# Forming the low parts of w2 and of later q/k weights on GpSimd, with w2 spread over the steps and the first MLP product four units sooner

## The chip, the cores and the metric

One core of a Trainium2 chip runs the kernel. Its engines are TensorE (PE in the profile; PEld is its weight load), VectorE (DVE), ScalarE (ACT), GpSimd (POOL) and SyncE (SP), which here issues every DMA. Each engine works through its own instruction stream in order; semaphores tie the streams together. The metric is the device time of one execution in microseconds (us), lower is better. The kernel before takes 837.43 us, the median of three runs (837.27 to 838.78).

## The reference, cut to what matters

Sequence 2048, width 640, 32 heads of 20, a causal window of 256, an MLP of width 1536 with squared relu. Attention and MLP both read the normalized input, and the MLP's output gates the attention's:

```python
xn = _layernorm(x, axis=-1)
s = _A_ref(xn, A_wqkv, A_wo)       # windowed softmax attention, then @ wo
g = _silu(_B_ref(xn, B_w1, B_b1, B_w2, B_b2))   # relu(xn @ w1 + b1)**2 @ w2 + b2
return x + s * g
```

Everything is float32. The kernel reaches that accuracy with half-precision products: each operand is scaled by a power of two and kept as a high part `hi` (rounded to f16) and a low part `lo` (what rounding left out), and a product is three matmuls, hi*hi, hi*lo and lo*hi.

## The kernel before, in words

**Three stages.** The first (to about 119 us) normalizes x, transposes it, makes the values, the first group of q and k, and the parts of w1. The second is one loop of 269 steps (line 1023, `for s in range(steps)`), which is written out by hand: on PE, ACT, DVE, GpSimd and SP the instructions run in the order in which the Python code issues them. The third, after the loop, is the output projection with the gate.

**A step.** Sixteen pairs of heads times sixteen blocks of 128 queries give 256 steps, plus 13 in which the pipeline runs out. Step s does, for different blocks: `scores` (PE, L558) and `maxima` (DVE, L569) of block s; `scores_t` (PE, L605), `exps` (ACT exponential, L610, then the two GpSimd selects L611 and L613 that zero what lies outside the window) of block s-10; `high` (ACT, L618) of block s-11; `low` (DVE, L624, the low part of the probabilities) of block s-12; `values` (PE, L638) of block s-13. So a select is read by the `high` of the next step, and that by the `low` of the step after.

**The filler.** Between these pieces `fill` (L1007) draws matmuls from one long generator, `filler` (L888), until a quota of cost is used up: 1.58 cost units a step (423.4 units over 268 steps). The generator is a list of units: 32 `group_unit`s (q and k of groups 1 to 4, four column blocks, 15 matmuls of 0.218 each, 3.27 units), 96 `hidden_unit`s (the first MLP product, 15 of 0.111, 1.665 units) and 96 `out_unit`s (the second product with w2, 12 of 0.138). Before, the first 16 group units stand alone and the other 16 are merged evenly with the 12 hidden units of the first token block (L892); then hidden units of the next block are merged with out units of this one. What a unit leaves in PSUM is moved out by an `evac`, run by `flush` in the step: for a group L80 on ACT and L81 on DVE, for a hidden unit L848 and L849 on ACT, L851 on DVE, L852 on GpSimd.

**Pieces of weights.** Weights that are needed later come in pieces of 128 x 640 f32. `piece` (L753) puts one in `queue`; `start_pieces`, called from `issue` twice a step, takes it out, starts its DMA into one of three `raw` buffers (RAW, L39) and puts it in `started`; `tick`, called once a step after `flush`, releases at most one piece, in order, two steps or more after its DMA was issued (AGE, L718), and runs its work. Tags name the pieces: "g2" to "g4" the q and k weights of a group (two pieces each, `split_s`), "s" the 17 that are only squared and summed for a scale (12 of w2, 5 of wo, L776), "20", "21", "22" the 12 of w2 (`split_s`), "o" those of wo. A tag in `shut` isn't released. `ensure` (L745) runs what is left of a tag at once.

**split_s** (L124) is the work of a weight piece: ACT writes `hi` with a scale (L125), and DVE computes src*scale - hi into `lo` in one instruction (L126).

**When.** Group g+1 is queued when `group_unit` enters (g, block 0, q), shut until (g, block 1, q). The squares are queued at (1, 1, q); `ensure("s")` and a small product of scales come at (3, 0, q); `second_scales` (L784: two small matmuls, a chain of small DVE and GpSimd instructions) and the queueing of w2 at (3, 1, q). The first `out_unit` calls `ensure` for w2's three tags.

Of the kernel before, what the change touches and what calls it, by code (L numbers as in the profile page):

```python
# [11 lines left out]
AF = mybir.ActivationFunctionType  # L12
ALU = mybir.AluOpType

P = 128
# [8 lines left out]
NB = 4  # L24
# [33 lines left out]
def attn_mlp_kernel(ctx: ExitStack, tc, x, wqkv, wo, w1, b1, w2, b2, out):  # L58
# [91 lines left out]
    def totals(name, r, acc, k=1):  # L150
        nc.tensor.matmul(r, onesf, acc, start=True, stop=True)
        t = col(name, k)
        nc.vector.tensor_reduce(out=t, in_=r.rearrange("p (k n) -> p k n", k=k), op=ALU.add, axis=mybir.AxisListType.X)  # L153
        nc.vector.tensor_scalar(t, t, TINY, None, ALU.max)
        return t

    sc_g, qkw, w1t, mlp, esc = {}, [], [], {}, []

# [559 lines left out]
    AGE = 2  # L718
    held = [0]
    shut = set()  # L720

    def start_pieces(n=3):
        k = 0
# [7 lines left out]
    def release(n, force=False):  # L731
        done = []
        while started and len(done) < n:
            tag, at_, go = started[0]
            if not force and (tag in shut or state[2] < at_ + AGE):
                break
            done.append(started.pop(0)[2])
        return done

# [10 lines left out]
                f()  # L750
                held[0] -= 1

    def piece(tag, src, go):  # L753
        def start():
            raw = wgt.tile([P, D], F32, tag="wraw", bufs=RAW, name="raw")
            if len(src.shape) == 3:
                raw = raw.rearrange("p (c n) -> p c n", n=src.shape[-1])
            nc.sync.dma_start(raw, src)
            return lambda: go(raw)
        queue.append((tag, start))  # L760

    def queue_group(g):
        r = {}
        for i, w in enumerate("qk"):
            hi, lo = (qkw[0][:, g % 2, i, j] for j in range(2))
            off = (0 if w == "q" else D) + g * P
            piece(f"g{g}", wqkv.rearrange("(c p) n -> p c n", p=P)[:, :, off:off + P], lambda raw, hi=hi, lo=lo, w=w: split_s(hi, lo, raw, sc_g[w]))
            r[w] = (hi, lo)
        return r

# [25 lines left out]
    def queue_w2(j):  # L796
        def go(raw, f):
            if len(w2t) == j:
                w2t.append(w2p.tile([P, SLOT], F16, name=f"w2_{j}") if j == 2 else bigp.tile([P, SLOT], F16, tag="big", name=f"w2_{j}"))
            hi, lo = (lin1(w2t, (2 * f + q) * D, D) for q in range(2))  # L800
            split_s(hi, lo, raw, mlp["s2"][:, f:f + 1])
        for f in range(4 * j, 4 * j + 4):
            piece(f"2{j}", w2[f * P:(f + 1) * P, :], lambda raw, f=f: go(raw, f))

# [4 lines left out]
    def group_unit(g, b, w):  # L809
        if w == "q":  # L810
            if b == 0:
                ensure(f"g{g}")
                if g + 1 < KC:
                    ws[g + 1] = queue_group(g + 1)
                    shut.add(f"g{g + 1}")
            if b == 1:
                shut.discard(f"g{g + 1}")
                if g == 1:
                    queue_squares()
            if g == KC - 2 and b == 0:  # L820
                ensure("s")
                weighted_squares()
            if g == KC - 2 and b == 1:
                second_scales()
                for j in range(3):
                    queue_w2(j)
# [61 lines left out]
    def filler():  # L888
        groups = [(group_unit, g, b, w) for g in range(1, KC) for b in range(NB) for w in "qk"]
        hid = [[(hidden_unit, n, fc) for fc in range(NF)] for n in range(nblk)]  # L890
        mlp2 = [[(out_unit, n, tt, nh, third) for tt in range(2) for nh in range(2) for third in range(3)] for n in range(nblk)]
        half = len(groups) // 2  # L892
        units = groups[:half] + merge(groups[half:], hid[0])
        for n in range(nblk - 1):
            units += merge(hid[n + 1], mlp2[n])
        units += mlp2[-1]
# [215 lines left out]
```

## Time and profile before

| what | value |
|---|---|
| runs of the kernel | 837.27, 837.43, 838.78 us |
| the profiled execution | 837.25 us, of which 835.5 us is the span from the first to the last instruction |
| granted TensorE clock | 0.998 of full speed |
| first and last score matmul (L558) | 119.2 and 727.3 us from the span's start |
| squares of pieces (L776) | 17, from 134.8 to 173.7 us |
| splits of w2 (L125 on ACT) | 12, from 223.6 to 255.3 us |

The page's first part gives the busy time of each engine over the span; a stage view (busy time between two moments, with instruction counts) is needed to see where an engine is short, since the stages differ. DVE's line L569 runs twice a step, and each of the two is followed by a readout that the profile counts under the same line, so four instructions of L569 are one step: that makes it a clock for the steps. Durations of neighbours on ACT and DVE overlap by about 0.1 us when they follow without a gap, so busy time is a little more than what an engine needs.

### The profile page before, as it was taken

What the parts mean: (1) busy time and instruction counts of PE and PEld (TensorE: products, weight loads), DVE (VectorE), ACT (ScalarE), POOL (GpSimd) and SP (SyncE); (2) the same over time, 40 slices, a digit from 0 to 9 for tenths busy, and PEclk for the clock granted to TensorE, in tenths of its full rate; (3) what the DMA queues carried; (4) which work ended last, traced back from release to release, by engine and by line L of the source; (5) the groups of instructions that cost most, each with busy time, mean ns of one, the idle gap of its engine ahead of it and who ended that gap; (6) DMA issues with size and microseconds to landing.
All of it is one profiled execution on the core that took longest, in us unless ns stands there. A gap on an engine that the chain in (4) does not pass through costs nothing.

```text
span 835.5 us, 24908 instructions
## 1 busy us (share of the span) xinstructions
PE 815.3 (98%) x9426; PEld 548.1 (66%) x9426; DVE 686.0 (82%) x1897; ACT 648.5 (78%) x1028; POOL 476.9 (57%) x874
## 2 busy tenths in 40 slices
PE   8999999999989999999999999999999999999998
PEld 6765563445545557777777777777777777767775
DVE  6777576788999889888988889888988889875665
ACT  5456455998898989898898989898898989893321
POOL 2000001446777768797878878797887878770000
PEclk9999999999999999999999999999999999999999
DMA  6894447765463332212121212211121131055873
GB/s 240 253 342 123 146 147 255 232 183 158 145 197 119 100 102 79 52 49 66 50 68 58 67 49 54 56 60 50 54 89 45 55 97 46 10 199 181 309 288 129
DMA packets 100497, 104.51 MB, mean 125 GB/s; under 512 B 42520, under 2 KB 72856, under 8 KB 100376
## 3 DMA queue, kind: packets, MB, share of 16 engines
q1 hardware_dynamic: 100376, 102.91, 39.5%
q8 instruction: 74, 1.21, 0.6%
q14 instruction: 47, 0.39, 0.2%
HBM read 65.67 MB, written 36.83 MB: 123 GB/s over the span
## 4 chain that ended last, share of the span: by engine, by line
PE 82%; ACT 7%; DVE 5%; issue 3%; DMA 2%; SPq 0%; DVEq 0%; ACTq 0%
PE hps L689 19%; PE yps L874 19%; PE wops L689 8%; PE ops L638 7%; PE vps L292 7%; PE sps L558 7%; PE qkps L689 7%; PE stps L605 3%; PE qkps L503 3%; ACT p L610 2%; DVE junk L569 2%; ACT ph L618 1%; PE otp L956 1%; PE tps L256 1%; DVE pl L624 1%
## 5 line engine op out<-in xcount | busy, mean ns | idle before, releaser
L610 ACT ACTIVATE p<-stps,ebias,esc 128x768 f32<-128x768 f32 (+2 forms) x256 | 242.3, 947 | 50.2 <-PE stps L605 42.4
L569 DVE CUSTOM_DVE_ANT_0 junk<-sps,mask 128x320 bf16<-128x320 f32 (+2 forms) x512 | 221.3, 469 | 54.8 <-PE sps L558 44.6
L624 DVE TENSOR_TENSOR pl<-p,ph 128x768 f16<-128x768 f32 (+2 forms) x256 | 243.6, 952 | 4.7 <-ACT ph L618 4.0
L611 POOL TENSOR_SCALAR_AFFINE_SELECT p<-p 128x256 f32<-128x256 f32 x256 | 171.4, 670 | 90.4 <-ACT p L610 87.8
L618 ACT ACTIVATE ph<-p 128x768 f16<-128x768 f32 (+2 forms) x256 | 203.2, 794 | 1.9 <-POOL p L613 0.9
L689 PE MATMUL hps<-xT,w 128*128 128x256 f16 x1440 | 188.8, 273 | 0.0
L874 PE MATMUL yps<-w,hh 128*128 128x320 f16 x1152 | 186.6, 300 | 0.0
L689 PEld LDWEIGHTS <-w 128*128 128x128 f16 x1440 | 133.3, 98 | 43.7 <-issue 23.7
L874 PEld LDWEIGHTS <-hh 128*128 128x128 f16 x1152 | 105.1, 98 | 55.6 <-issue 21.8
L689 PE MATMUL qkps<-xT,qkw 128*128 128x512 f16 x480 | 117.0, 381 | 0.8 <-DVE w_t L153 0.8
L613 POOL TENSOR_SCALAR_AFFINE_SELECT p<-p 128x256 f32<-128x256 f32 x224 | 110.5, 493 | 0.0
L558 PE MATMUL sps<-ks,qs 60*64 60x320 f16 (+2 forms) x1024 | 86.1, 313 | 6.5 <-DVE mt L569 5.9
L638 PE MATMUL ops<-vp,ph 128*128 128x41 f16 x1440 | 89.8, 181 | 0.0
L638 PE MATMUL ops<-vp,pl 128*128 128x41 f16 x1440 | 89.5, 181 | 0.0
L638 PEld LDWEIGHTS <-ph 128*128 128x128 f16 x1440 | 84.6, 96 | 6.2 <-issue 0.6
L638 PEld LDWEIGHTS <-pl 128*128 128x128 f16 x1440 | 78.9, 96 | 5.8
L605 PE MATMUL stps<-qs,ks 62*64 62x320 f16 (+4 forms) x1024 | 79.6, 291 | 2.3 <-ACT p L610 2.0
L574 POOL CAST mp<-mt 128x8 f16<-128x8 f32 x64 | 44.1, 689 | 62.2 <-DVE mt L569 61.6
L689 PEld LDWEIGHTS <-qkw 128*128 128x128 f16 x480 | 41.6, 98 | 53.4 <-issue 11.7
L852 POOL TENSOR_TENSOR hh<-sq,hh 128x256 f16<-128x256 f32 x96 | 67.6, 704 | 13.0 <-DVE sq L851 9.3
L292 PE MATMUL vps<-wv,xT 128*128 128x320 f16 x480 | 70.0, 302 | 3.2 <-ACT xT L261 1.6
L689 PE MATMUL wops<-wo,oT 128*128 128x320 f16 x480 | 66.7, 299 | 0.8 <-ACT oT L121 0.8
(150 smaller groups left out, 974.8 us busy)
## 6 DMA issues: line engine op xcount, KB each, us to landing
ks<-k_d SPq DMA_DIRECT2D x64, 120.0 KB
qs<-q_d SPq DMA_DIRECT2D x64, 120.0 KB
raw<-in_B_w_dram SPq DMA_DIRECT2D x24, 320.0 KB
v_d<-vt SPq DMA_DIRECT2D x8, 656.0 KB
vp<-v_d SPq DMA_DIRECT2D x16, 328.0 KB
xt<-in_A_x_dram SPq DMA_DIRECT2D x16, 320.0 KB
k_d<-shm SPq DMA_DIRECT2D x20, 256.0 KB
q_d<-shm SPq DMA_DIRECT2D x20, 256.0 KB
```

The costliest lines, as they stand in the source:

```text
L292: nc.tensor.matmul(ps, xT[b][:, xp, c, t * P:(t + 1) * P], wv[wp][:, c, nh * HALF:(nh + 1) * HALF], start=n == 0, stop=n == 3 * KC - 1)
L558: nc.tensor.matmul(ps[HB * j:HB * (j + 1), :nk], qs[i][rows_, q0:q0 + HB], ks[i][rows_, k0:k0 + nk], start=True, stop=True)
L569: nc.vector.tensor_tensor_reduce(out=junk[:, :nk], in0=ps[:, :nk], in1=mk, scale=1.0 / MAX_UNIT, scalar=-3.0e38, op0=ALU.add, op1=ALU.max, ...
L605: nc.tensor.matmul(ps[HB * j:HB * (j + 1), hh, c0:c1], ks[i][rows_, kb * P + HB * j:kb * P + HB * (j + 1)], qs[i][rows_, kb * P + c0:kb * ...
L610: nc.scalar.activation(p32[:, :, :n], ps[:, :, :n], AF.Exp, scale=esc[0], bias=ebias)
L611: nc.gpsimd.affine_select(p32[:, :, 0:P], p32[:, :, 0:P], pattern=[[0, 2], [1, P]], compare_op=ALU.is_ge, fill=0.0, base=0, channel_multip ...
L613: nc.gpsimd.affine_select(p32[:, :, 2 * P:], p32[:, :, 2 * P:], pattern=[[0, 2], [-1, P]], compare_op=ALU.is_gt, fill=0.0, base=0, channel ...
L618: nc.scalar.activation(ph[:, :, :n], p32[:, :, :n], AF.Copy)
L624: nc.vector.tensor_sub(pl[:, :, :n], p32[:, :, :n], ph[:, :, :n])
L638: nc.tensor.matmul(ot[:, q % 4, hh, :], t[:, hh, (q - k) * P:(q - k + 1) * P], vp[:, k // 4, k % 4, hh, :], start=m == 1, stop=m == 2 * le ...
L689: nc.tensor.matmul(ps, a, b_, start=j == 0, stop=j == n - 1)
L874: nc.tensor.matmul(ps, hh[:, hp, tt * P:(tt + 1) * P], lin1(w2t, (2 * fc + wp) * D + nh * HALF, HALF), start=fc == 0 and j == 0, stop=fc = ...
```

## The change

- A new function `split_p` makes the low part in two GpSimd instructions, in place of DVE's one: the raw piece is multiplied by its scale in place, then `hi` is subtracted. ACT's part stays. It is used for the two pieces each of groups 2, 3 and 4 and for the 12 of w2: 18 pieces. Other splits keep `split_s`.
- `release` keeps the step in which a kind of piece (first letter of its tag) was last released and lets the next go only `pace` steps later: 3 for w2, 2 for squares once the step is past 10, 1 for the others.
- Group g+1 is queued at (g, block 1, q), no longer at block 0, never shut, and put ahead of what is in the queue.
- The first 12 group units stand alone, and the other 20 are merged with the first 12 hidden units.

```diff
+    def split_p(hi, lo, src, sc):
+        nc.scalar.activation(hi, src, AF.Copy, scale=sc)
+        nc.gpsimd.tensor_scalar(src, src, sc, 1.0, ALU.mult, ALU.mult)
+        nc.gpsimd.tensor_sub(lo, src, hi)
...
+    last = {}
+
+    def pace(kind):
+        return 3 if kind == "2" else 2 if kind == "s" and state[2] > LAG else 1
...
-            if not force and (tag in shut or state[2] < at_ + AGE):
+            if not force and (tag in shut or state[2] < at_ + AGE or state[2] < last.get(tag[0], -9) + pace(tag[0])):
                 break
+            last[tag[0]] = state[2]
             done.append(started.pop(0)[2])
...
-    def piece(tag, src, go):
+    def piece(tag, src, go, ahead=False):
...
-        queue.append((tag, start))
+        if ahead:
+            queue.insert(sum(t == tag for t, _ in queue), (tag, start))
+        else:
+            queue.append((tag, start))
...
-            piece(f"g{g}", wqkv.rearrange("(c p) n -> p c n", p=P)[:, :, off:off + P], lambda raw, hi=hi, lo=lo, w=w: split_s(hi, lo, raw, sc_g[w]))
+            piece(f"g{g}", wqkv.rearrange("(c p) n -> p c n", p=P)[:, :, off:off + P], lambda raw, hi=hi, lo=lo, w=w: split_p(hi, lo, raw, sc_g[w]), True)
...
-            split_s(hi, lo, raw, mlp["s2"][:, f:f + 1])
+            split_p(hi, lo, raw, mlp["s2"][:, f:f + 1])
...
                 ensure(f"g{g}")
+            if b == 1:
                 if g + 1 < KC:
                     ws[g + 1] = queue_group(g + 1)
-                    shut.add(f"g{g + 1}")
-            if b == 1:
-                shut.discard(f"g{g + 1}")
                 if g == 1:
                     queue_squares()
...
-        half = len(groups) // 2
-        units = groups[:half] + merge(groups[half:], hid[0])
+        first = 3 * NB
+        units = groups[:first] + merge(groups[first:], hid[0])
```

## The prediction

> **What bounds the kernel now.** I read the page's head first, then the stage view restricted to L569 (four instructions are one step), then the same stages for all engines, then the chain of waits in three of them.
>
> ```profile
> span 835.5 us, 24908 instructions
> PE 815.3 (98%) x9426; PEld 548.1 (66%) x9426; DVE 686.0 (82%) x1897; ACT 648.5 (78%) x1028; POOL 476.9 (57%) x874
> ```
>
> PE looks full, but a waiting matmul also counts as busy, so the steps have to be timed. The columns are window, its length, DVE's busy time in L569 and the count:
>
> ```profile
> 135.00:183.00 48.00, 15.72 (x72) 1.00 0.75 237
> 183.00:208.00 25.00, 9.41 (x44) 1.00 0.58 168
> 213.00:220.00 7.00, 1.72 (x8) 1.00 0.33 106
> 213.00:258.00 45.00, 12.84 (x60) 1.00 0.55 168
> 258.00:319.00 61.00, 23.16 (x105) 1.00 0.36 104
> 400.00:700.00 300.00, 112.19 (x515) 1.00 0.22 61
> ```
>
> A step is 300/(515/4) = 2.33 us from 400 on, and the same before: 2.27 from 183 to 208, 2.32 from 258 to 319. Two stretches are slow. 135 to 183 (steps 8 to 25) takes 2.67 a step: 48 - 18 x 2.33 = **6.1 us** too much. 213 to 258 (steps 39 to 53) takes 3.00: 45 - 15 x 2.33 = **10.0 us** too much, of which 7 - 2 x 2.33 = 2.3 lies in its first two steps, where the scales of w2 are made. Who is short there, by the stage view of all engines (PE, PEld, DVE, ACT, POOL busy):
>
> ```profile
> 135.00:183.00 48.00, 43.66 (x412) 20.29 (x412) 36.23 (x105) 43.66 (x80) 18.50 (x44) 1.00 0.75 237
> 183.00:208.00 25.00, 25.00 (x307) 12.98 (x304) 21.80 (x66) 21.61 (x31) 16.57 (x34) 1.00 0.58 168
> 213.00:258.00 45.00, 40.33 (x455) 23.20 (x453) 44.48 (x117) 41.80 (x63) 34.11 (x54) 1.00 0.55 168
> 258.00:319.00 61.00, 60.57 (x730) 34.48 (x727) 54.25 (x161) 53.88 (x83) 43.77 (x81) 1.00 0.36 104
> 400.00:700.00 300.00, 300.00 (x4144) 215.73 (x4144) 267.04 (x788) 269.73 (x412) 244.25 (x431) 1.00 0.22 61
> ```
>
> In the first slow stretch ACT is the fullest (43.66 of 48), in the second DVE (44.48 of 45). The chain of waits says the same; its summary for 135:183, for 220:260 and for 400:700:
>
> ```profile
> by line: issue 20.0%; ACT p L610 16.4%; DMA raw<-in_B_w_dram 14.5%; ACT unread L776 13.7%; ACT ph L618 12.9%; DMA k_d<-shm 7.3%; ACT shm L80 6.0%; DVE junk L569 4.3%; DVE qkw L126 1.9%; ACT qkw L125 1.8%; PE qkps L689 1.6%; SPq L669 1.0%; P
> ```
> ```profile
> by line: issue 27.4%; DVE junk L569 20.7%; DVE w L126 16.8%; DVE pl L624 12.9%; ACT p L610 4.9%; ACT w L125 3.5%; DVE shm L81 2.3%; PE qkps L689 1.9%; DVE mt L569 1.4%; DVE sq L851 1.4%; DVE mrow L588 1.3%; ACT shm L80 1.2%; ACT relu L848 1
> ```
> ```profile
> by line: PE hps L689 35.7%; PE yps L874 35.5%; PE ops L638 12.0%; PE sps L558 10.8%; PE stps L605 5.4%; PE sps L584 0.6%
> ```
>
> From 400 on it is PE alone. So the change can win 6.1 + 7.7 us at most, and whatever stall it adds comes off that.
>
> **When the pieces run.** Both schedules follow from the counters in the code: 1.58 units of filler a step, one release a step, AGE 2, the paces. Before: squares at steps 6 to 22, g3 at 23 and 24, g4 at 40 and 41, w2 at 42 to 53, one every step; the trace agrees (the 12 L125 of w2 run from 223.6 to 255.3 us). After: g2 at 6 and 7, squares at 8, 9, 10, then every second step from 12, g3 at 25 and 26, the last two squares forced together at 36; `second_scales` at 41 instead of 39 (four hidden units stand ahead of it, not two); g4 at 44 and 45; w2 at 46, 49, ... 79. The first out unit is due after 32 x 3.27 + 13 x 1.665 = 126.3 units, step 79 both times, so w2 is just ready: nothing is forced there.
>
> **Part 1: squares, later g2, hidden units sooner (steps 8 to 36).**
>
> ```profile
> ACT unread L776 <- DMA raw<-in_B_w_dram: 6.1, 4, 2.6
> ```
> ```profile
> 131.05 0.41 SPq L758 DMA_DIRECT2D raw<-in_B_w_dram  x1
> ```
>
> The g2 loads move from steps 0 and 1 to 4 and 5. There they take the places in SP's queue and the buffers of the first squares' loads (131.05), so ACT waits for g2's landing instead of the squares': I take 0, with -2.6 (one such wait more) and +2.6 (one less) as the ends. Then ACT's work over the 29 steps: 43.66 + 21.61 = 65.3 us now. Two more hidden units fall into it and about one group unit out:
>
> ```profile
> L848 ACT ACTIVATE relu<-hps,m,m 128x256 f32<-128x256 f32 x96 | 53.4, 557 | 0.0
> ...
> L849 ACT ACTIVATE hh<-relu 128x256 f16<-128x256 f32 x96 | 40.0, 417 | 3.0
> ...
> L80 ACT ACTIVATE shm<-qkps 128x512 f16<-128x512 f32 x40 | 23.7, 594 | 15.3 <-PE qkps L503 7.7 <-PE qkps L689 7.6
> ```
>
> 2 x 0.97 - 0.59 = 1.4, so 66.7 us of ACT, while PE needs 29 x 2.33 = 67.6, and the stretch takes 73 now. ACT at 95% gives 70.2; at 90%, its share from 400 to 700, 74; at PE's rate 67.6. I take 95%, between them: **gain 3.0**, ends -1 and +5.4.
>
> **Part 2: DVE's low parts go.** In 213:258 fourteen L126 run:
>
> ```profile
> L126 DVE SCALAR_TENSOR_TENSOR w<-raw,m_sf,w x12: 862/871/1297, 224.9 to 257.2; 128x640 f16<-128x640 f32 x12
> ```
>
> 14 x 0.87 = 12.2 us, more than the 7.7 of stall beside the scales. **Gain 7.7** if nothing else is late. The 2.3 of the scales stay: `second_scales` isn't changed, only moved. What is late next is ACT: 53.88/26.25 = 2.05 a step from 258 on, plus a piece every third step:
>
> ```profile
> L125 ACT ACTIVATE w<-raw,m_sf x12: 812/824/832, 223.6 to 255.3; 128x640 f16<-128x640 f32 x12
> ```
>
> 2.05 + 0.82/3 = 2.33, just PE's rate (less in truth, as neighbours' durations overlap by 0.1). I charge nothing for it beside the next part, which stalls the same steps.
>
> **Part 3: what GpSimd takes over.** No row shows a 128x640 operation there. The nearest, min/median/max in ns:
>
> ```profile
> L613 POOL TENSOR_SCALAR_AFFINE_SELECT p<-p x224: 397/403/1210, 143.4 to 747.7; 128x256 f32<-128x256 f32 x112
> ```
> ```profile
> L106 POOL TENSOR_SCALAR_AFFINE_SELECT mask<-mask x1: 292/292/292, 2.8 to 2.8; 128x128 f32<-128x128 f32 x1
> ```
> ```profile
> L852 POOL TENSOR_TENSOR hh<-sq,hh x96: 664/667/1470, 208.4 to 730.5; 128x256 f16<-128x256 f32 x96
> ```
> ```profile
> L575 POOL TENSOR_TENSOR mp<-mt,mp x64: 201/204/850, 127.0 to 729.6; 128x8 f16<-128x8 f32 x64
> ```
>
> One input: (397 - 292)/128 = 0.82 ns an element, so 640 take 397 + 384 x 0.82 = 0.71 us. Two inputs: (664 - 201)/248 = 1.87 ns, so 664 + 384 x 1.87 = 1.38 us, and 0.1 between the two, since the second reads the first's result. **A piece is 2.2 us** of GpSimd; the ends are 1.6 (both at one-input rate) and 2.9 (both at two-input rate).
>
> From step 44 to 79 (36 steps, 83.9 us at PE's rate) lie 14 pieces. GpSimd's present work is 43.77/26.25 = 1.667 us a step, waits inside its instructions included: 36 x 1.667 + 14 x 2.2 = 60.0 + 30.8 = 90.8 us, 6.9 more than there is. A lag can build up to about 2.33 - 0.79 = 1.5 us first, as a step's two selects (0.79) are read a step later by L618. So **5.4 us come back** as stall; with a piece of 1.6 us it would be 0, with 2.9 it would be 36 x 1.667 + 14 x 2.9 - 83.9 - 1.5 = 15.2. Queued behind a piece's first instruction, which waits for ACT's `hi`, are the next step's selects; `high` on ACT waits for those, and the exponential, PE's `scores_t` and DVE's `low` follow. The third load after a piece waits on SP until GpSimd is done with the buffer, with pair loads and row writes behind it that are needed two steps later or more: 0.
>
> The sum: 837.25 - 3.0 - 7.7 + 5.4 = 832.0 us for the profiled execution; the median lies 0.2 above that one: **832.1 us**. Nothing changes before step 4, or in the last stage.
>
> **The rivals.** What decides is how GpSimd and DVE get in each other's way. The trace shows it:
>
> ```profile
> 228.89 0.95 DVE L624 TENSOR_TENSOR pl<-p,ph 128x768 f16<-128x768 f32 x1
> 229.76 1.30 DVE L126 SCALAR_TENSOR_TENSOR w<-raw,m_sf,w 128x640 f16<-128x640 f32 x1
> ```
> ```profile
> 228.90 1.47 POOL L852 TENSOR_TENSOR hh<-sq,hh 128x256 f16<-128x256 f32 x1
> ```
>
> L852 (0.66 alone) starts just after L624 and takes 0.8 us longer, as if it began near L624's end (229.84). The L126 that starts while L852 runs (to 230.37) takes 1.30, not 0.87. Each blocks the other, whichever is second.
>
> - *GpSimd has room.* The waits in its 1.667 a step come partly from the L126 that go, and from free choice of place; with all waits out, the 90.8 would fall below 83.9. Then only parts 1 and 2 count: 837.4 - 10.7 = 826.7. Against it: from 400 on there is no L126, and GpSimd is still at 244.25/300.
> - *Half the pieces are blocked once by an L624* (0.8 us): 14 x 0.4 = 5.6 more, come-back 11.0, and 837.4 - 10.7 + 11.0 = 837.7: DVE's stall has changed its name.
> - *Slower: GpSimd becomes the bound.* Every piece is blocked once: 11.2 more, come-back 16.6, 843.3. It decides against the change from a piece of (83.9 + 1.5 + 10.7 - 60.0)/14 = 2.6 us on, waits included. For it: one L624 comes every 2.33 us, and a piece lasts 2.2. Against it: a piece that delays DVE's L624 isn't delayed by it, and L624 waits for ACT anyway.
> - *The change doesn't do what it says*: the pieces are forced at step 79 after all, or the scales wait. 837.4.
>
> The Trainium skill (SBUF — State Buffer, section "Who interferes with whom") says that a DVE instruction with two SBUF inputs contends with a GpSimd instruction that reads SBUF, and that the one which starts first holds the shared port for its whole length. The rows above agree with it in both directions. Taken strictly, it forbids GpSimd any overlap with L624 and so speaks for the third case, 843.3.
>
> **How the numbers follow.** Forecast (829 to 834.7) 0.45; GpSimd has room (824.5 to 829) 0.20; half blocked (834.7 to 839) 0.20, a quarter of it still faster by 0.2%; bound by GpSimd (over 839) 0.12; no effect 0.03. This kernel's runs can tell 0.2%, 1.7 us, from no change, so faster is below 835.8 and slower above 839.1: faster 0.45 + 0.20 + 0.05 = 0.70, same 0.15 + 0.03 = 0.18, slower 0.12. The range runs from 825 (no come-back, part 1 at 4.7 of its 5.4) to 839 (half blocked, part 1 at 1.7); the dearest piece, 15.2 of come-back, gives 841.9 and is left out with the third rival.
>
> **What would show it.** Right: steps of 2.33 to 2.45 us by L569 from step 10 on, no stretch at 3.00; GpSimd near 95% of the time from about 228 to 312 us; its subtract near 1.4 us and multiply near 0.7 at their shortest; ACT's L618 waiting for GpSimd, which it hardly does now. Wrong: GpSimd still under 85% there (then 827), a minimum of the two instructions over 2.9 together, L624 growing past 1.5 us on average, or PE waiting in a new place, such as g2's landing at about 131 to 137 us or the two squares at step 36.

## The result, and the profile after

The changed kernel takes **847.51 us** (median of four runs, 846.40 to 848.44), the kernel before 837.35 on the same chip (836.97 to 838.78). The ratio is 1.0121, 95% interval 1.0109 to 1.0133: 10.1 us slower, where 832.1 was forecast in a range of 825 to 839. The profiled execution took 848.3 us; the granted clock was 0.992 (0.998 before).

The page's head, after:

```profile
span 846.6 us, 24915 instructions
PE 819.5 (97%) x9426; PEld 548.8 (65%) x9426; DVE 686.2 (81%) x1879; ACT 647.9 (77%) x1028; POOL 516.9 (61%) x910
```

GpSimd has 40 us more than before (516.9 against 476.9): 18 pieces of some 2.3 us. DVE's busy time hasn't fallen (686.2 against 686.0) although 18 instructions are gone from it. That is a first sign that what stayed on DVE got longer.

The clock for the steps is DVE's maxima line again, L574 now (L569 before), four instructions a step. The stage view after, restricted to that line (window, length, busy, count), and then the two windows of before that were not shown yet:

```profile
135.00:183.00 48.00, 16.73 (x76) 0.96 0.74 224
183.00:206.00 23.00, 7.68 (x37) 1.00 0.65 194
206.00:228.00 22.00, 7.16 (x32) 1.00 0.39 115
228.00:330.00 102.00, 31.62 (x147) 0.97 0.46 133
411.00:711.00 300.00, 112.23 (x513) 1.00 0.22 61
```
```profile
183.00:206.00 23.00, 8.98 (x43) 1.00 0.55 159
206.00:228.00 22.00, 6.70 (x32) 1.00 0.48 142
```

Up to 206 us the kernel before has made 72 + 43 = 115 instructions, 28.75 steps, the changed one 76 + 37 = 113: it gains a step up to 183 us and gives back one and a half after it, where hidden units come sooner and two squares are forced together. Edges of a window cut instructions, so half a step is the limit of this reading. The timeline of VectorE says it more closely. These are the moments, in us from the span's start, at which the first maxima of a step begin:

| kernel | step 8 | step 37 | step 44 | step 80 | step 255 |
|---|---|---|---|---|---|
| before | 135.11 | 208.15 | 228.07 | 318.86 | 727.64 |
| after | 135.44 | 208.78 | 228.65 | 329.71 | 738.70 |

Steps 8 to 36 take 73.0 us before and 73.3 after, steps 37 to 43 take 19.9 in both, and the 36 steps 44 to 79 take 90.8 before and 101.1 after. So 10.3 of the 11.1 us between the two profiled executions are lost in steps 44 to 79. The pieces of w2 do run when they were meant to, at steps 46, 49, ... 79. The stage view of all engines for 228 to 330 us (PE, PEld, DVE, ACT, POOL), before and after:

```profile
228.00:330.00 102.00, 98.25 (x1202) 57.86 (x1200) 94.43 (x262) 93.34 (x139) 77.53 (x134) 1.00 0.42 127
```
```profile
228.00:330.00 102.00, 92.87 (x1064) 51.80 (x1063) 88.92 (x224) 85.55 (x129) 94.53 (x142) 0.97 0.46 133
```

After, 147/4 = 36.75 steps fit into these 102 us, 2.78 us a step; PE's rate is 2.33. PE, DVE and ACT all do less than before in the same time, GpSimd alone does more: 94.53 of 102. From step 90 to step 255 both take the same 386.2 us. Who waits for whom from 228 to 330 us, from the view of waits (engine and line, releaser: us in total, times, longest):

```profile
ACT ph L623 <- POOL p L618: 10.1, 8, 2.6
...
PEld L589 <- POOL mp L580: 4.9, 2, 3.4
PE sps L589 <- POOL mp L580: 4.7, 2, 3.3
```

ACT's `high` (L623) waits 10.1 us for GpSimd's selects, and PE twice for `mp` (L580): the maxima of two steps, which GpSimd splits into high and low parts so that PE can transpose them (L589). What a piece and its neighbour take there, from the groups of instructions (busy, mean ns, idle before); VectorE's `low` (L624, L629) before and then after, and after it GpSimd's lines:

```profile
L624 DVE TENSOR_TENSOR pl<-p,ph 128x768 f16<-128x768 f32 x37 | 37.0, 1001 | 0.1
```
```profile
L629 DVE TENSOR_TENSOR pl<-p,ph 128x768 f16<-128x768 f32 x32 | 41.3, 1291 | 4.5 <-ACT ph L623 4.5
...
L616 POOL TENSOR_SCALAR_AFFINE_SELECT p<-p 128x256 f32<-128x256 f32 x37 | 20.0, 539 | 3.5 <-ACT p L615 2.1 <-DMA qs<-q_d 1.3
L160 POOL TENSOR_TENSOR w<-raw,w 128x640 f16<-128x640 f32 x12 | 18.9, 1574 | 1.0
...
L159 POOL TENSOR_SCALAR raw<-raw,m_sf 128x640 f32<-128x640 f32 x12 | 10.3, 855 | 0.2
L656 POOL TENSOR_TENSOR on<-osb 128x160 f32<-128x160 f32 x9 | 8.3, 926 | 0.9 <-ACT osb L650 0.9
...
L159 POOL TENSOR_SCALAR raw<-raw,g_s 128x640 f32<-128x640 f32 x2 | 2.3, 1140 | 0.0
```

A piece of w2 is 0.86 + 1.57 = 2.43 us on average. VectorE's `low` takes 1.29 us on average, 1.00 before: 0.29 more in each of some 36 steps is 10.4 us, most of what the 14 instructions of 0.87 us took that DVE was spared there (12.2). At one place everything comes together, three pieces in a row (two of a group, one of w2). The timeline of GpSimd, DVE and PE there:

```profile
235.28 1.48 POOL L159 TENSOR_SCALAR raw<-raw,g_s 128x640 f32<-128x640 f32 x1
236.85 1.40 POOL L160 TENSOR_TENSOR qkw<-raw,qkw 128x640 f16<-128x640 f32 x1
238.21 1.17 POOL L659 TENSOR_TENSOR on<-on,rs 128x160 f32<-128x160 f32 x1
239.33 0.59 POOL L616 TENSOR_SCALAR_AFFINE_SELECT p<-p 128x256 f32<-128x256 f32 x1
239.88 0.40 POOL L618 TENSOR_SCALAR_AFFINE_SELECT p<-p 128x256 f32<-128x256 f32 x1
240.27 0.79 POOL L159 TENSOR_SCALAR raw<-raw,m_sf 128x640 f32<-128x640 f32 x1
241.15 1.39 POOL L160 TENSOR_TENSOR w<-raw,w 128x640 f16<-128x640 f32 x1
242.49 0.91 POOL L579 CAST mp<-mt 128x8 f16<-128x8 f32 x1
243.49 0.20 POOL L580 TENSOR_TENSOR mp<-mt,mp 128x8 f16<-128x8 f32 x1
```
```profile
240.00 0.08 DVE L574 DVE_READ_ACCUMULATOR2_ANT mt<- 128x1 f32 x1
241.19 2.17 DVE L629 TENSOR_TENSOR pl<-p,ph 128x768 f16<-128x768 f32 x1 [1.11 <-ACT ph L623]
```
```profile
243.75 0.29 PE L589 MATMUL sps<-identh,mp 128*128 128x128 f16 x1 [3.25 <-POOL mp L580]
```

DVE has the maxima at 240.08. GpSimd is free for them at 242.49, behind the w2 piece. L629 starts at 241.19, just behind the piece's subtraction, and ends at 243.36: 0.82 us after that one's end, a little less than its own length. And L579, a copy of 8 columns that takes 0.2 us elsewhere, takes 0.91 and so ends behind L629. PE stands for 3.25 us.

### The profile page after: what moved, and what is told of

It is laid out like the page before. It is cut to its first block, busy times and chain, and to the rows that moved or that the text cites. A ratio compares the mean times of both kernels' runs of the same rounds, so it can differ in the third digit from the quotient of the medians.

```text
span 846.6 us, 24915 instructions
## 1 busy us (share of the span) xinstructions
PE 819.5 (97%) x9426; PEld 548.8 (65%) x9426; DVE 686.2 (81%) x1879; ACT 647.9 (77%) x1028; POOL 516.9 (61%) x910
## 3 DMA queue, kind: packets, MB, share of 16 engines
q8 instruction: 74, 1.21, 0.6%
## 4 chain that ended last, share of the span: by engine, by line
PE 77%; ACT 8%; POOL 6%; issue 4%; DVE 3%; DMA 2%; SPq 0%; POOLq 0%; DVEq 0%; ACTq 0%
PE yps L886 18%; PE hps L694 18%; PE wops L694 8%; PE vps L297 7%; PE ops L643 7%; PE sps L563 6%; PE qkps L694 5%; PE stps L610 3%; PE qkps L508 3%; ACT p L615 3%; ACT ph L623 1%; POOL raw L159 1%; POOL w L160 1%; PE otp L968 1%; PE tps L261 1%
## 5 line engine op out<-in xcount | busy, mean ns | idle before, releaser
L574 DVE CUSTOM_DVE_ANT_0 junk<-sps,mask 128x320 bf16<-128x320 f32 (+2 forms) x512 | 221.4, 469 | 58.8 <-PE sps L563 46.5
L629 DVE TENSOR_TENSOR pl<-p,ph 128x768 f16<-128x768 f32 (+2 forms) x256 | 257.4, 1005 | 8.4 <-ACT ph L623 7.8
L623 ACT ACTIVATE ph<-p 128x768 f16<-128x768 f32 (+2 forms) x256 | 203.2, 794 | 15.8 <-POOL p L618 13.1
L616 POOL TENSOR_SCALAR_AFFINE_SELECT p<-p 128x256 f32<-128x256 f32 x256 | 166.8, 652 | 69.8 <-ACT p L615 67.0
L694 PE MATMUL qkps<-xT,qkw 128*128 128x512 f16 x480 | 119.0, 386 | 0.0
L618 POOL TENSOR_SCALAR_AFFINE_SELECT p<-p 128x256 f32<-128x256 f32 x224 | 108.3, 483 | 0.0
L563 PE MATMUL sps<-ks,qs 60*64 60x320 f16 (+2 forms) x1024 | 84.4, 315 | 1.3 <-DVE mt L574 0.9
L579 POOL CAST mp<-mt 128x8 f16<-128x8 f32 x64 | 45.2, 706 | 46.8 <-DVE mt L574 46.5
```

The lines of the kernel that those rows point to most:

```text
L563: nc.tensor.matmul(ps[HB * j:HB * (j + 1), :nk], qs[i][rows_, q0:q0 + HB], ks[i][rows_, k0:k0 + nk], start=True, stop=True)
L574: nc.vector.tensor_tensor_reduce(out=junk[:, :nk], in0=ps[:, :nk], in1=mk, scale=1.0 / MAX_UNIT, scalar=-3.0e38, op0=ALU.add, op1=ALU.max, ...
L616: nc.gpsimd.affine_select(p32[:, :, 0:P], p32[:, :, 0:P], pattern=[[0, 2], [1, P]], compare_op=ALU.is_ge, fill=0.0, base=0, channel_multip ...
L618: nc.gpsimd.affine_select(p32[:, :, 2 * P:], p32[:, :, 2 * P:], pattern=[[0, 2], [-1, P]], compare_op=ALU.is_gt, fill=0.0, base=0, channel ...
L623: nc.scalar.activation(ph[:, :, :n], p32[:, :, :n], AF.Copy)
L629: nc.vector.tensor_sub(pl[:, :, :n], p32[:, :, :n], ph[:, :, :n])
```

## The experiments

A ratio is to the kernel before in the same comparison; 0.1% is 0.84 us. Unless said otherwise an edit is made to the changed kernel.

### Which of the four parts costs

**All low parts back on VectorE**, with the new order, pace and first product:

```diff
-... lambda raw, hi=hi, lo=lo, w=w: split_p(hi, lo, raw, sc_g[w]), True)
+... lambda raw, hi=hi, lo=lo, w=w: split_s(hi, lo, raw, sc_g[w]), True)
-            split_p(hi, lo, raw, mlp["s2"][:, f:f + 1])
+            split_s(hi, lo, raw, mlp["s2"][:, f:f + 1])
```

> The changed kernel with every low part back on DVE; pace, queue order and the earlier first MLP product stay. Theory LOAD (GpSimd is overfull in steps 44 to 79 and the port it shares with DVE makes each piece dearer) and theory MAX (a piece holds up the two small GpSimd instructions on the maxima, for which PE's transposition waits in order) both say that the loss goes and the spreading is left: 828 to 832 us. If the pace or the order themselves cost, it stays at 837 or above.

Measured: 836.81 us, ratio 0.9993 (0.9981 to 1.0005). Without the move to GpSimd the rest of the change is worth nothing that can be told, and the move costs 1.28%, 10.7 us.

**Only the group pieces back on VectorE** (the first of the two edits):

> The changed kernel with the six pieces of q/k groups on DVE again, the twelve of w2 stay on GpSimd. MAX: the two long waits of PE (at 136 and 240 us, where pieces of a group stand close together) and the half clock after them go, about 2.8 + 3.3 + 3 us: 838 to 839. LOAD: 2 of the 14 pieces between steps 44 and 79 go, 14% of the overload: 845 to 846.

843.63 us, 1.0079 (1.0062 to 1.0096). So w2's twelve pieces cost 0.86%, 7.2 us, and the groups' six the other 3.5. In the profiles, steps 44 to 79 alone take 97.3 us here and 101.1 in the changed kernel, so the 3.5 are mostly those of group 4's two pieces, which come just ahead of w2's first.

**The maxima's two small instructions on VectorE** (`nc.vector` in place of `nc.gpsimd` in L579 and L580), so that PE's transposition no longer waits behind a piece:

> The changed kernel with the two small instructions on the maxima (128x8) moved from GpSimd to DVE. MAX: PE's waits ahead of the transposition (2.8, 0.6, 3.3, 1.6 and 0.7 us in the trace of the changed kernel) go, and the half clock after the two longest with them: 836 to 839 us. LOAD: GpSimd is as full as before, less 0.2 us a step group: 844 to 847 us, and the waits turn up at ScalarE's L623 or PE's score products.

846.51 us, 1.0114 (1.0091 to 1.0137): hardly anything, although PE's waits for GpSimd's `mp` are gone and with them the stretches of half clock (below). Steps 44 to 79 take 101.8 us. In the view of waits for 228 to 330 us the other wait is still there, nearly as long (10.1 us in the changed kernel):

```profile
ACT ph L623 <- POOL p L618: 9.4, 8, 2.2
```

**What of the rest is good and what bad.** First the group's pieces queued at block 0 again, but ahead and not shut, with the low parts on VectorE:

```diff
             if b == 0:
                 ensure(f"g{g}")
-            if b == 1:
                 if g + 1 < KC:
                     ws[g + 1] = queue_group(g + 1)
+            if b == 1:
                 if g == 1:
```

> All low parts on DVE as in e1_dve_low, pace and the earlier first MLP product kept; the weights of group g+1 are queued at block 0 again, ahead and not shut, so g2's loads start at step 0 and g4 is done at steps 38 and 39, before the scales. If ScalarE's wait for g2's landing in steps 6 to 9 (2.8 us late in e1's trace at step 8, with 3.4 us of half clock) is what ate the gain of the spread squares: 833 to 834.5 us. If the stretch was full of ScalarE's work anyway: 836 to 837.

835.44 us, 0.9974 (0.9964 to 0.9985). Then also the first product where it was (`first = 4 * NB`), so that only the pace and the early queueing are left:

> e6_pace_first with 16 group units alone, as before the change: pace and queue order without the earlier first MLP product. If four hidden units sooner overfill ScalarE in steps 27 to 36 while squares still run: 1 to 2 us faster than e6. If they lighten steps 44 to 79, where w2 runs: 1 to 2 us slower than e6.

**831.98 us**, 0.9932 (0.9919 to 0.9946): this one beats both kernels. And the first product four units sooner alone, in the kernel before (`half = 3 * NB`):

> The kernel before with only the first MLP product four units sooner. No part of the loss is expected here: 836 to 838.5 us. Over 839 it would be part of the loss.

838.89 us, 1.0014 (1.0005 to 1.0023). So the four parts: pace and early queueing give 5.7 us, the first product sooner takes 3.5 back (1.2 in the kernel before), late queueing 1.6, GpSimd 10.7. What the pace does is seen by the maxima in the kernel of 831.98 us (72, 43, 32 and 165 in the kernel before):

```profile
135.00:183.00 48.00, 17.11 (x80) 1.00 0.73 221
183.00:206.00 23.00, 7.60 (x36) 1.00 0.68 200
206.00:228.00 22.00, 8.14 (x36) 1.00 0.45 145
228.00:330.00 102.00, 36.09 (x168) 1.00 0.41 121
```

Two steps are gained up to 183 us, but 1.75 of them are given back by 206, since the squares that were moved out of the first stretch run in the second (the last at 197.8 us, before at 173.7). The time is won after that. The stages by the first maxima of a step, in us of the one profiled execution of each kernel:

| kernel | steps 8 to 36 | steps 37 to 43 | steps 44 to 79 |
|---|---|---|---|
| before | 73.0 | 19.9 | 90.8 |
| first product sooner alone | 73.4 | 19.1 | 92.7 |
| pace, early queueing | 73.0 | 17.1 | 88.9 |
| the same, first product sooner | 70.8 | 21.1 | 89.6 |
| all low parts on VectorE | 67.8 | 19.9 | 90.8 |
| changed | 73.3 | 19.9 | 101.1 |

Steps 8 to 36 say little: with all low parts on VectorE step 8 began some 5 us later than in the other kernels, and four kernels that issue the same instructions up to step 41 took 71.8 to 73.0 us in them. What the first product sooner costs beside the pace lies in steps 37 to 43. There PE waits 2.1 us for sums for the scales of wo (L151) and runs 3.4 us at half clock after it; without it the granted clock is 1.00 there.

### What of a piece costs

**A piece that reads nothing**: four fills of the same size, of about the same length, in place of the two instructions.

```diff
-        nc.gpsimd.tensor_scalar(src, src, sc, 1.0, ALU.mult, ALU.mult)
-        nc.gpsimd.tensor_sub(lo, src, hi)
+        nc.gpsimd.memset(src, 0.0)
+        nc.gpsimd.memset(src, 0.0)
+        nc.gpsimd.memset(src, 0.0)
+        nc.gpsimd.memset(lo, 0.0)
```

> The changed kernel with the two GpSimd instructions of a piece replaced by four memsets, three over the raw piece and one into the low part, so the low parts of w2 and of q/k groups 2 to 4 are left out (zero). GpSimd is held for about the same 2.2 us, but reads nothing. If it is the shared port: DVE's low parts of the probabilities (L629 in the changed kernel) no longer wait for pieces, 838 to 842 us. If it is the time alone, by LOAD or by MAX: 845 to 848 us.

840.38 us, 1.0037 (1.0022 to 1.0052). The rows of 228 to 330 us:

```profile
L631 DVE TENSOR_TENSOR pl<-p,ph 128x768 f16<-128x768 f32 x36 | 37.0, 1028 | 3.6 <-ACT ph L625 3.4
L160 POOL MEMSET raw<- 128x640 f32 x14 | 8.8, 631 | 0.8
...
L162 POOL MEMSET w<- 128x640 f16 x12 | 7.6, 631 | 0.0
```

4 x 0.63 = 2.52 us, no shorter than the piece, and never blocked (625 to 632 ns each), and DVE's `low` takes 1.03 us beside it, not 1.29. So without reads the same length costs 0.44% over the kernel with the low parts on VectorE, 3.7 us; with them 0.84% more, 7.0 us; steps 44 to 79 take 94.5 us, against 90.8 and 101.1. ACT's waits for the selects don't tell the two apart: 10.1 us in 224 to 330 us here, 11.9 in the changed kernel. The Trainium skill (SBUF — State Buffer, "Who interferes with whom") says that DVE's two-input instruction contends with a GpSimd instruction that reads SBUF and not with one that only writes it; these rows agree.

**A shorter piece.** First the multiplication left out, only the subtraction stays (the line with `tensor_scalar` deleted):

> The changed kernel without the multiplication on GpSimd, so the low parts of w2 and groups 2 to 4 are those of the unscaled piece: scaling left out. A piece holds GpSimd and the port for one instruction of 1.4 us instead of two of 2.3 together. LOAD as an overload beyond a threshold: 14 x 0.9 = 12.6 us of GpSimd less in steps 44 to 79 is more than the whole loss there, 837 to 840 us. If each piece costs by how long the port is read, the loss against e1 shrinks in proportion, 10.7 x 1.4/2.3 = 6.5: 843.

835.15 us, 0.9967 (0.9955 to 0.9980), even below the kernel with all low parts on VectorE. 0.8 us less in a piece takes away the whole loss, 1.54%. Steps 44 to 79 take 91.1 us, as with the low parts on VectorE (90.8), although DVE's `low` is still long there, 1.17 us on average: that it is longer is not by itself what costs. Then the multiplication replaced by one fill, which takes 0.63 us and reads nothing:

> The changed kernel with the multiplication replaced by one memset over the raw piece (so the low parts of w2 and groups 2 to 4 are only minus the high part). A piece holds GpSimd for 0.63 + 1.4 us, near the 0.8 + 1.4 of the changed kernel, but reads for 1.4 only, as in e9_subtract_only (835.15 us). If time held decides: 844 to 847. If time that it reads decides: 835 to 838. If both count: 839 to 842.

841.02 us, 1.0043 (1.0028 to 1.0058): midway between the two, where both the time held and the time that is read count. A fill that reads nothing costs 0.76%, 6.4 us, over the subtraction alone.

**Fewer pieces, and only w2's.** In the kernel of 831.98 us, w2's low parts on GpSimd, all twelve and then every other one:

```diff
-            split_s(hi, lo, raw, mlp["s2"][:, f:f + 1])
+            split_p(hi, lo, raw, mlp["s2"][:, f:f + 1])
```
```diff
-            split_s(hi, lo, raw, mlp["s2"][:, f:f + 1])
+            (split_p if f % 2 else split_s)(hi, lo, raw, mlp["s2"][:, f:f + 1])
```

> e7_pace_only (pace and early queue, all low parts on DVE, 831.98 us) with the twelve low parts of w2 on GpSimd by the two instructions. LOAD: GpSimd is overfull from step 42 to 77 as in the changed kernel, so it loses what e4 lost against e1, about 7 us: 837 to 840. If the loss needs the change's order of units or its queueing, it stays within 2 us of e7.

> e7_pace_only with every second piece of w2 on GpSimd (six), the others on DVE. LOAD as a threshold: 6 x 2.3 us fit into GpSimd's spare time in steps 42 to 77 (about 24 us by the prediction's budget), and DVE has 5 us less to do: 830 to 832.5. If each piece on GpSimd costs its share: half of what e10 loses, 835 to 836.

838.75 us, 1.0017 (1.0006 to 1.0027), and 836.42, 0.9991 (0.9981 to 1.0001). Twelve pieces cost 0.85%, 7.1 us, as in the changed kernel; six cost 0.59%. So there is no threshold of GpSimd's whole work below which a piece would be free: a piece that has six steps to itself still costs 0.8 us. It is longer there, 1.10 + 1.80 = 2.9 us on average in 228 to 330 us, where DVE forms the other low parts.

### Burst or load

Two theories were left. *Burst*: one uninterrupted stretch of GpSimd work that is longer than a step's slack holds up the next step's selects. *Load*: GpSimd's total is what counts. The two instructions of a piece one step apart keep the total and shorten the stretch:

```diff
-        nc.gpsimd.tensor_sub(lo, src, hi)
+        second.append(lambda: nc.gpsimd.tensor_sub(lo, src, hi))
...
+    def subtract():
+        while second:
+            second.pop(0)()
+
     def tick():
+        subtract()
...
```

> The kernel after, with the two instructions of every GpSimd piece issued one step apart: the multiplication (0.80 us) in its step, the subtraction (1.40 us) at the start of the next step. Work, bytes read and GpSimd's total are the same. Theory of the burst (what costs is the length of one uninterrupted stretch of GpSimd work against the slack of a step, some 1.5 us): no stretch is longer than 1.4 us any more, so the time falls to about that of the kernel without the multiplication, 837 to 839 us, and ScalarE's waits for the selections in 224 to 330 us fall from 11.9 to about 4 us. Theory of the load (what costs is GpSimd's total time or its use of the port): 846 to 847 us, the waits as in after.

845.09 us, 1.0093 (1.0078 to 1.0108). And the same in the kernel with the pace and w2 on GpSimd:

> The kernel with the early queueing and the pace alone (831.98 us with all low parts on VectorE), with w2's low parts on GpSimd as in the run that took 838.75 us, but with each piece's multiplication and subtraction one step apart. Burst: 832 to 833 us. Load: 838 to 839 us.

838.14 us, 1.0007 (0.9995 to 1.0018). The time falls by 0.28% and 0.10% only, so the length of one stretch doesn't explain the whole cost. But burst isn't refuted by it, since the split also brings something new. The waits in 224 to 330 us of this last kernel, and GpSimd and SyncE ahead of one of them:

```profile
ACT ph L624 <- POOL p L619: 4.7, 9, 0.8
...
PE stps L611 <- DMA qs<-mrow: 3.4, 2, 1.8
```
```profile
242.69 1.40 POOL L160 TENSOR_TENSOR w<-raw,w 128x640 f16<-128x640 f32 x1
```
```profile
244.12 0.33 SPq L776 DMA_DIRECT2D raw<-in_B_w_dram  x1
244.55 1.28 SPq L675 DMA_DIRECT2D qs<-mrow  x2
```

ACT's waits for the selects do fall, from 11.4 us with each piece in one step to 4.7; in the changed kernel's variant they fall from 11.9 to 8.9, where burst foretold about 4. In their place PE's `scores_t` now waits for the DMA that brings the maxima (`mrow`) into `qs`: 3.4 us here, 2.6 in the changed kernel's variant, nothing in these 106 us in the two kernels without the split. The lines show how: `mrow` was written by 238.59 us, but SyncE issues in order and stood at the load of a piece, whose buffer came free only with the subtraction's end at 244.09. In 228 to 330 us SyncE waits 33.5 us for the subtractions, 17.4 without the split. The groups show what else grew, in the changed kernel's variant:

```profile
L160 POOL TENSOR_TENSOR w<-raw,w 128x640 f16<-128x640 f32 x12 | 19.8, 1652 | 0.0
...
L159 POOL TENSOR_SCALAR raw<-raw,m_sf 128x640 f32<-128x640 f32 x12 | 13.3, 1107 | 0.0
```

The piece grew from 2.43 to 2.76 us, perhaps because two starts meet DVE's `low` twice. A split without the late buffer was not run. In the changed kernel itself SyncE waits 15.8 us for w2's subtractions, but the engines wait for a DMA only once, 1.3 us, so SyncE's queue isn't what costs there.

Then load: other work taken off GpSimd, the pieces left as they are. The out units' addition goes (the multiplication that follows reads `osb`):

```diff
-            nc.gpsimd.tensor_add(on, osb[:, :, 0:DH], osb[:, :, DH:2 * DH])
...
-                nc.gpsimd.tensor_mul(on, on, rs.unsqueeze(2).to_broadcast([P, 8, DH]))
+                nc.gpsimd.tensor_mul(on, osb[:, :, 0:DH], rs.unsqueeze(2).to_broadcast([P, 8, DH]))
```

> The kernel after, with the addition on GpSimd in every out unit (on, 128x160, some 0.7 us) left out, so that the low parts' share of the outputs is missing; the pieces stay as they are. Theory of the load (GpSimd is full from step 44 to 84, 107 us of work in 109.7, so every microsecond that it is spared there comes off the time): ten such additions lie in that stretch, 7 to 8 us, so 839 to 841 us. Theory that a piece itself, by its length or by its reads beside VectorE's, costs a fixed stall: the pieces are the same, 846 to 848 us.

843.91 us, 1.0072 (1.0056 to 1.0089). The control, where GpSimd has no pieces:

> The same addition left out of the kernel with the early queueing and the pace alone, all low parts on VectorE (831.98 us). Load: GpSimd has 82 us of work in 97.3 there and isn't the bound, so nothing follows, 831.5 to 832.5 us. Were the addition dear for another reason (its port use, the row writes behind it), this kernel would gain from its absence as well, several us.

831.49 us, 0.9928 (0.9913 to 0.9943), no difference to 0.9932. So the same addition is worth 0.49% where GpSimd is full and nothing where it isn't: GpSimd's time is one thing that is short. But it is half of what load alone foretold. Are these two bounds that hide each other? Both edits together, in both kernels, and the missing corner:

> The kernel after with both edits: the pieces' two instructions one step apart, and the addition of the out units left out. Theory of two bounds (a stall comes where either the lag that one piece leaves in its own step or the total of GpSimd's work over the three steps of the pace exceeds what there is; taking one away leaves the other): now neither holds, so together they give far more than their sum (2.4 + 3.6): 835 to 839 us. Theory of the sum (each microsecond on GpSimd and each long stretch costs its own share): 847.5 - 2.4 - 3.6, 841 to 842 us.

> The kernel with the early queueing and the pace, w2's low parts on GpSimd, each piece over two steps, and the addition of the out units left out. Two bounds: neither holds, 831.5 to 834 us, as with the low parts on VectorE. Sum: 838.14 less some 0.6 to 1, 837 to 838 us.

> As the last one, but each piece in one step (the kernel of 838.75 us with the addition left out). Two bounds: the lag of a piece in its own step stays, less the 0.2 us a step that the addition took, 836 to 837.5 us. Sum: 837 to 838 us. It is the fourth corner beside 838.75, 838.14 and the run above.

Ratios in per cent to the kernel before (plain, split over two steps, addition left out, both):

| kernel | plain | split | less | both |
|---|---|---|---|---|
| changed | +1.21 | +0.93 | +0.72 | +0.42 |
| pace, w2 on GpSimd | +0.17 | +0.07 | -0.15 | -0.49 |

In the first row the two add up (0.28 + 0.49 = 0.77 against 0.79). In the second both together give more than the sum (0.66 against 0.42), but the uncertainty of that difference is as large (the four half-intervals, 0.10, 0.12, 0.11 and 0.18, in quadrature: 0.26). So the sum fits in the first and is not excluded in the second; the theory of two bounds isn't shown. It isn't excluded either: the uncertainty in the first row is no smaller, and the split kernels have PE's new wait for `mrow`.

How far GpSimd's work explains the steps is seen over all kernels, the two of the comparison among them. For 228 to 330 us, GpSimd's busy time and the time of a step, each divided by the steps that the maxima give:

| kernel | GpSimd a step | us a step |
|---|---|---|
| pace, addition left out | 1.79 | 2.41 |
| low parts on VectorE | 1.86 | 2.44 |
| before | 1.88 | 2.47 |
| before, first product sooner | 1.93 | 2.53 |
| pace, all on VectorE (831.98) | 1.95 | 2.43 |
| the same, first product sooner | 1.96 | 2.43 |
| pace, every other of w2 | 2.17 | 2.53 |
| pace, w2, addition left out | 2.26 | 2.53 |
| subtraction alone | 2.33 | 2.49 |
| pace, w2, split, addition left out | 2.34 | 2.49 |
| changed, addition left out | 2.39 | 2.68 |
| changed, split, addition left out | 2.42 | 2.60 |
| a fill and the subtraction | 2.47 | 2.62 |
| pace, w2 on GpSimd | 2.47 | 2.62 |
| pace, w2, split | 2.47 | 2.55 |
| changed, groups on VectorE | 2.47 | 2.67 |
| fills instead of a piece | 2.48 | 2.62 |
| changed, maxima on VectorE | 2.49 | 2.76 |
| changed | 2.57 | 2.78 |
| changed, split | 2.58 | 2.70 |

Up to 2.33 of GpSimd's work, PE's rate, a step takes 2.41 to 2.53; above it a step is 0.1 to 0.3 longer than GpSimd's own work, in each pair less where the pieces are split. The row of the kernel that the table turns on, the subtraction alone, in the stage view:

```profile
228.00:330.00 102.00, 98.77 (x1207) 57.91 (x1205) 95.25 (x253) 95.59 (x144) 95.61 (x145) 1.00 0.46 134
```

GpSimd is as full as in the changed kernel (95.61 against 94.53), but the steps in this time are 41, not 36.75: here a full engine that just keeps up costs next to nothing (41.75 steps with all low parts on VectorE).

**What stays open** is how the price of a piece divides between its total, its length and the blocking of DVE. Of 10.3 + 2.3 = 12.6 us of multiplication taken out of the pieces in 228 to 330 us, 10.0 came back in steps 44 to 79; of 8.3 us of the addition, 2.1 (4.1 by the runs, with an uncertainty of 1.7). Pieces at other moments of a step, which might miss L629, were not tried.

## Why the prediction failed

**Part 3 is the step that failed**, and in its second half. The price of a piece was right: 2.2 us forecast, 0.79 + 1.39 unblocked in the timeline above (with the gap between them 2.27), 2.43 on average. So was the work: 36 steps with 14 pieces were to be 90.8 us for GpSimd, and 94.53/36.75 x 36 is 92.6. What failed is the overlap: GpSimd was taken to be busy without a gap, and on top of it "A lag can build up to about 2.33 - 0.79 = 1.5 us first", so that only "**5.4 us come back**". Steps 44 to 79 took 101.1 us in place of 83.9: 17.2 came back. In 228 to 330 us GpSimd stood idle for 102 - 94.53 = 7.5 us, which the forecast put at nothing, 3.5 of it before the first select, whose input was late in its turn. Idle time, 1.8 us more work and the credit of 1.5 that didn't show are 10.8 of the 11.8 us between 17.2 and 5.4. The kernel with every other piece fits this: six steps lie between two of its pieces, more than enough to let a lag run down, and each still costs 0.8 us. What a step waits for while a full GpSimd stands idle isn't shown. The signs that the forecast named for being right came mostly true (GpSimd at 93% of the time, its two instructions at 0.79 and 1.39 us at their shortest, ACT waiting for GpSimd), but the steps took 2.78 us, not 2.33 to 2.45: those signs spoke of the work, not of the time.

Not all of the 17.2 is the move's. With all low parts on VectorE the same steps take 90.8 us, 6.9 over PE's rate without a piece on GpSimd; 10.3 are the move's.

The forecast's own third rival had 16.6 us of come-back, at a chance of 0.12; that size and the place were nearly right, and its 843.3 us fell short because it took the gains of parts 1 and 2 with it. Its mechanism, that a piece is blocked once by L624, was half of it: a piece grew by 0.2 us, not by 0.8, but DVE's `low` grew from 1.00 to 1.29. The argument against it, "a piece that delays DVE's L624 isn't delayed by it, and L624 waits for ACT anyway", let DVE's delay go for nothing. By the fills reading isn't free; but with the subtraction alone `low` grew as well, to 1.17, and no time was lost, so DVE's delay is not by itself what cost. The rule of the Trainium skill that was set beside it (SBUF — State Buffer, "Who interferes with whom") was the better guide: the timeline shows L629 at 2.17 us beside the subtraction, and pieces of fills, which read nothing, cost 7.0 us less.

"**Queued behind a piece's first instruction … are the next step's selects**" left out the maxima's `mp` (L579, L580), on which PE's transposition waits. That wait is real, 3.25 us at 243.75 and 2.75 at 139.45, but moving it away gained only 0.07%, which can't be told from none. The term put at 0 beside it, loads that wait on SyncE for a buffer, was right from 228 to 330 us: 15.8 us of such waits led to one wait of 1.3 us for a DMA.

**Part 1, a gain of 3.0, came to nothing**: steps 8 to 36 took 73.3 us, 73.0 before, where 70.2 was forecast. The term that failed is "I take 95%" for ACT. From 135 to 206 us ACT was busy for 63.47 of 71 us, 89%, as before (63.30), and 92% (65.22) with the pace and early queueing alone, where the stretch was 73.0 us again. So spreading the squares moved the stall from the first half of the stretch into the second and hardly shortened it. The end of the range, "at 90%, … 74", was the better estimate. Two more things went against it. The g2 loads, taken as "0, with -2.6 … and +2.6", land late, and GpSimd's first pieces with them. ACT, GpSimd and PE after, from the timeline:

```profile
135.77 0.83 ACT L158 ACTIVATE qkw<-raw,g_s 128x640 f16<-128x640 f32 x1 [3.26 <-DMA raw<-in_A_wqkv_dram]
```
```profile
136.70 0.80 POOL L159 TENSOR_SCALAR raw<-raw,g_s 128x640 f32<-128x640 f32 x1 [9.17 <-DMA k_d<-shm]
137.58 1.39 POOL L160 TENSOR_TENSOR qkw<-raw,qkw 128x640 f16<-128x640 f32 x1
138.92 0.19 POOL L579 CAST mp<-mt 128x8 f16<-128x8 f32 x1
139.19 0.20 POOL L580 TENSOR_TENSOR mp<-mt,mp 128x8 f16<-128x8 f32 x1
```
```profile
139.45 0.23 PE L589 MATMUL sps<-identh,mp 128*128 128x128 f16 x1 [2.75 <-POOL mp L580]
```

GpSimd stands at the piece from 127.5 on, since its order is fixed and `hi` isn't there (the releaser named, a DMA, isn't it: L159 starts 0.1 us after L158's end); the maxima, queued behind it, come at 138.92. Late queueing is 1.6 us in all, by the two kernels that differ in it (the uncertainty of that difference is 1.3). The other is the hidden units sooner, priced at 1.4 us of ACT's work in steps 8 to 36 and found at 3.5 beside the pace, in steps 37 to 43. The two squares forced together at the end, at steps 36 and 37, were not tried apart.

**Part 2, a gain of 7.7**, wasn't seen. With the subtraction alone DVE is spared the same instructions and GpSimd keeps up, and still steps 37 to 79 take 110.9 us, 110.7 before. That kernel is 0.26% faster than the one with all low parts on VectorE, but ahead of step 44, not after it. The lump on DVE gave way in part to the pace, without GpSimd: with pace and early queueing alone steps 37 to 79 take 106.0 us, so 4.7 of the 10.5 over PE's rate are gone. What holds the rest isn't shown; from 228 to 330 us PE, DVE, ACT and GpSimd are all busy for 95 us or more with the subtraction alone, so "I charge nothing" for ACT may be part of it.

The account, for the profiled execution (832.0 forecast, 848.3 measured, 16.3 apart): 11.8 us in steps 44 to 79; 3.3 in steps 8 to 36 (3.0 gained in the forecast, 0.3 lost); 1.3 in steps 37 to 43 (7 x 2.33 + 2.3 = 18.6 forecast, 19.9 taken); 0.3 ahead of step 8 and 0.2 after step 80. That is 16.9; the kernel before stood 10.5 us over PE's rate in steps 37 to 79, where the forecast had 10.0, which is 0.5 of the difference.

## What to carry to other kernels

Work moved to an engine that isn't on the critical path isn't free up to the point where that engine is full, and the engine's total alone doesn't price it: here the subtraction alone (1.5 us a piece, GpSimd at 2.33 us a step) cost nothing, the whole piece 0.6 us each and more, also where GpSimd had only 2.17 us a step. An engine that is budgeted as full still stands idle where its own inputs are late, so a budget of work against time is a lower bound. Price what the moved instruction does to its neighbours, too: reading beside a two-input VectorE instruction made that one 0.29 us longer, from 1.00, which took back most of what VectorE had been spared. Take a change of several parts apart before judging it: the pace and the early queueing alone, without the move, give 831.98 us. And count a gain over the whole stretch: the two steps won up to 183 us were given back by 206.

## What the hardware showed that was not expected

PE's clock fell by half after its two waits of some 3 us. The stage view of PE after, in two windows (length, busy, granted clock):

```profile
140.50:143.90 3.40, 3.40 (x15) 0.50 0.59 154
243.00:249.70 6.70, 5.95 (x34) 0.50 0.55 202
```

The records of the clock have 3.41 us at half after the wait of 2.75, and 6.83 after the one of 3.25, once and twice the same length. The Trainium skill (TensorE: Matmul & The Clock Gate, Part 1) says that the clock is set by a free-running window of 3413 ns; the lengths agree. The trace agrees less with a row of its table, "after ≥1 idle window": the waits were shorter than one. The cost is bounded by half of the 10.2 us; the kernel without these two waits was 1 us faster, which can't be told from none.
